# Gate sums moved to TensorE, row loads to SyncE's queue, and the small steps of the maxima spread over ScalarE and GpSimd

## The chip, the cores and the metric

The kernel runs on one NeuronCore of a Trainium2 chip. The core has four computing engines, each with its own in-order queue of instructions: TensorE (PE in the profile, its weight loads PEld) multiplies matrices into PSUM, VectorE (DVE), ScalarE (ACT) and GpSimd (POOL) work elementwise and reduce. SyncE (SP) issues DMAs; ScalarE and GpSimd can issue DMAs too, and an instruction that issues one waits in that engine's queue like any other. The metric is the device time of one execution in microseconds. A program on one core has no second core to wait for, so the time is the span of this core's instructions and a little around it.

## The reference

For an input x of 2048 rows and 512 columns the kernel computes a gated mix of two layers, in float32:

```python
g = sigmoid((x * gate_w).sum(-1, keepdims=True))
q, k, v = split(x @ wqkv)              # 32 heads of 16 columns each
a = (softmax(q @ k.T * 16 ** -0.5) @ v) @ wo        # per head, then the output matrix
b = Cr @ (x @ Wr.T) - Ci @ (x @ Wi.T)               # real part of a Fourier transform over rows and columns
out = g * a + (1 - g) * b
```

Wr, Wi (512 x 512) and Cr, Ci (2048 x 2048) are inputs. The weights wqkv and wo are scaled up by 64, so the scores of the softmax are large: each row's maximum has to be known before the exponentials.

## The kernel before, in words

**Precision.** Most matrix products run on float32 operands that are split into two rounded halves, `hi` and `lo` (type F32R). A product is then three products, hi*hi, hi*lo and lo*hi, collected in PSUM. `split` (line 336) makes the halves: ScalarE copies to `hi`, another engine subtracts to get `lo`. `halves_of` (line 185) gives each product as two matmuls on 64 rows each, into two PSUM banks that are added at the evacuation.

**Stages.** The order of the instructions is written out by hand; no planner moves them. All of the following runs in one stream of TensorE:

1. Projections to q and k, transposed (`project_t`, line 465): 32 tiles of 128 x 512, the first nine in the list `order` (line 548). Their operands come from the transposed input xT, loaded into four tiles `raws` in quarters of 512 columns, and from the first columns of wqkv. Every tile is evacuated from PSUM (ScalarE, then DVE or POOL), split into `eh` and `el`, and stored to DRAM (`q_d`, `k_d`).
2. Projections to the values (`project_s` with `wv`, 16 tiles, about 115.7 to 184.4 us). In the same stretch the gate's sums are made: for each block of 128 rows, `load_xn` (line 569) loads x through SP, `gate_sum` (line 573) multiplies it with the gate's row, broadcast to all partitions in `gb`, on POOL, and ScalarE sums the product over its columns into `z`. `gates` (line 589) turns z into g and 1 - g.
3. The two column transforms (`project_s` with `wr`, then `wi`, 16 tiles each, to about 314.5 us), stored to DRAM (`ab_d`), and `fold_keys` (line 412), which makes sums and differences of key columns.
4. The row transforms (88 groups of 24 matmuls, to about 683 us). Their coefficients `craw` are loaded by SP eight groups ahead into five buffers, and split by POOL (`prepare`, line 363).
5. The attention of 16 pairs of heads, one after another, with the rest of the row transforms and the output matrix beside it.

**Scans beside the stages.** The maxima of the scores are found beside stages 1 to 4. A scan multiplies a block of queries with a block of keys (line 139 for the first pair, line 158 after it); DVE, or ScalarE and DVE together (a fold: lines 162 and 164), reduce the result to the maxima `mx`. Every step of three products advances a count of slots (`beside`, line 292). Work is put a number of slots later by `after(n, f)`, and a scan is given out every few slots (PACE 3.9, BESIDE 2.72, PART 2.07 slots a scan), independent of the time that passes.

**Row loads.** The scans of a pair of heads need rows of q and k, which `row_loads` (line 93) brings from DRAM into two tiles of the ring `stk` (six buffers) with eight DMAs. `load_scan_beside` (line 284) puts them seven slots apart, beginning 28 scans before the pair starts (24 for the second pair). For the first pair they are issued by SP, for the other pairs by ScalarE. In the row transforms a pair's 64 scans are 132 slots, a group of 24 matmuls 12 slots.

**The end of a pair.** `shift` (line 167) reduces the maxima once more, transposes them (both DVE), splits them into `hi` and `lo` (lines 181 and 182, both DVE, 128 x 32 elements), and SP stores both. The five parts come three slots after the pair's last scan and then every four slots. For one pair, `PART_PAIR`, the tile of maxima is first filled by a memset on POOL (line 155).

**Evacuation of the natural-order tiles.** `project_s` (line 495) multiplies one bank of the result by a sign into `tx` on ScalarE. For odd tiles after the first 64 scans DVE adds the other bank from PSUM; for the others ScalarE evacuates it too (`ty`, line 506) and POOL adds.

Of the kernel before, what the change touches and what calls it, by code (L numbers as in the profile page):

```python
# [10 lines left out]
F32 = mybir.dt.float32  # L11
# [7 lines left out]
P = 128  # L19
# [33 lines left out]

def build(tc, x, xT, wqkv, wo, wrT, wiT, cr, ci, gate, out):
    nc = tc.nc
    with ExitStack() as ctx:
# [88 lines left out]
        def scan_folded(n, j, bank, pool):  # L145

            p, i = SEQ[n]  # L150
            qb, c = i // 4, i % 4
            if i == 0 and j == 0:
                new_maxima(p)
                if p == PART_PAIR:
                    nc.gpsimd.memset(mx[p], -3.0e38)
            qs, ks = scanned[p]
            b, ps = 64 * j, bank(f"{'dk'[c % 2]}{j}")
            nc.tensor.matmul(ps, qs[b:b + 48, qb * P:(qb + 1) * P], ks[b:b + 48, c * 512:(c + 1) * 512],  # L158
                             start=True, stop=True)
            if c % 2 == 0:  # L160
                fold[j] = pool.tile([P, 512], F32, tag=f"fold{j}", name="fold")
                nc.scalar.activation(fold[j], ps, AF.Relu)  # L162
            else:
                nc.vector.tensor_tensor_reduce(out=fold[j], in0=ps, in1=fold[j], scale=1.0, scalar=-3.0e38,  # L164
                                               op0=ALU.add, op1=ALU.max, accum_out=mx[p][:, j, qb, c // 2:c // 2 + 1])

        def shift(p):

# [5 lines left out]
            def store():  # L174
                for n, s in enumerate((hi, lo)):
# [4 lines left out]
                    lambda: nc.vector.transpose(t, m),  # L180
                    lambda: nc.vector.tensor_copy(hi, t),
                    lambda: nc.vector.tensor_sub(lo, t, hi.bitcast(F32)),
                    store]
# [71 lines left out]
        with ExitStack() as pf:  # L255
# [28 lines left out]
            def load_scan_beside(p):  # L284
                scanned[p], loads = row_loads(p, nc.scalar if p else nc.sync, kf_d if p else k_d)
                for n, load in enumerate(loads):
                    after(7 * n, load)
# [4 lines left out]
            def beside():  # L292
# [6 lines left out]
                while seen[0] < FRONT and pace[1] >= 1.0:  # L299
# [16 lines left out]
                    if done is not None and SEQ[done][1] == SCANS - 1:  # L316
                        for d, part in enumerate(shift(SEQ[done][0])):
                            maxima.append(part)
# [64 lines left out]
            with ExitStack() as px:  # L383
# [28 lines left out]
                def fold_keys(f, g):  # L412

                    a, b = (ep.tile([P, 512], F32, tag="el", name="fa") for _ in range(2))
                    c = 2 * g
# [30 lines left out]
                def difference(f, c, s):  # L446
# [5 lines left out]
                    kept.clear()  # L452
                    hi = ep.tile([P, 512], F32R, tag="dh", name="dh")
                    lo = a.bitcast(F32R)
# [10 lines left out]
                def project_t(w, dst, f, c, ps=None):  # L465
# [6 lines left out]
                    hi = ep.tile([P, 512], F32R, tag="eh", name="eh", bufs=3)  # L472
                    lo = ep.tile([P, 512], F32R, tag="el", name="el")
                    nc.scalar.copy(tx, ps[0])
# [20 lines left out]
                def project_s(w, t, sign, use):  # L495
# [5 lines left out]
                    nc.scalar.mul(tx, ps[0], sign)  # L501
                    if beds and t % 2 and t < NB - 1:
                        after(4, use, t, tx, ps[1], nc.vector.tensor_add if sign > 0 else nc.vector.tensor_sub)
# [20 lines left out]
                for d in range(ND):  # L524
                    nc.sync.dma_start(raws[d][:, q4[0]], xT[d * P:(d + 1) * P, q4[0]])
                    nc.sync.dma_start(rq[d][:, near], wqkv[d * P:(d + 1) * P, near])
                load_cols(1, near)
                for c in range(1, NC):
                    load_x(c)
                for i in range(2):  # L530
                    load_cols(i, far)
                nc.sync.dma_start(ones_d.rearrange("a (b c) -> (a b) c", c=32), ones)
                gb = ep.tile([P, D], F32, tag="gb", name="gb", bufs=1)
                after(200, nc.sync.dma_start, gb, gate.to_broadcast([P, D]))

# [6 lines left out]
                for d in range(ND):  # L542
# [3 lines left out]
                    for c in range(1, NC):  # L546
                        after(24 * c - 6 + 4 * d, split_x, d, c)
                order = [(wq, q_d, 0, 0), (wk, k_d, 0, 0), (wq, q_d, 1, 0)]
                order += [(w, dst, 0, c) for c in range(1, NC) for w, dst in ((wq, q_d), (wk, k_d))]
                for n, (w, dst, f, c) in enumerate(order):  # L550
                    lead = s1() if n in (0, 2, 4, 6) else None
                    project_t(w, dst, f, c, lead and (lead[:, 0, :], lead[:, 1, :]))
                after(22, load_scan_beside, 0)
                after(84, scan_at, PACE)
# [11 lines left out]
                wr = new_cw()  # L566
                xn = {}

                def load_xn(t):
                    xn[t] = rp.tile([P, D], F32, tag="raw", name="xn")  # L570
                    nc.sync.dma_start(xn[t], x[t * P:(t + 1) * P, :])

                def gate_sum(t):
                    xg = ep.tile([P, D], F32, tag="el", name="xg")
                    nc.gpsimd.tensor_mul(xg, xn.pop(t), gb)
                    after(7, lambda: nc.scalar.activation(xg, xg, AF.Copy, accum_out=z[:, t:t + 1]))

                def to_values(t, tx, ps, add):
# [3 lines left out]
                for t in range(NB):  # L582
                    load_xn(t)
                    after(30 if t < NB - 1 else 18, gate_sum, t)
                    if t == 2:
# [525 lines left out]
```

## Time and profile before

| | |
|---|---|
| time, median of 3 runs | 1749.48 us (1747.13 to 1753.26) |
| the profiled execution | 1751.22 us, its span 1749.4 us |
| instructions | 36091 |
| TensorE busy | 1720.8 us (98%) |
| ScalarE busy | 1518.9 us (87%) |
| VectorE busy | 1098.3 us (63%) |
| GpSimd busy | 676.6 us (39%) |
| mean granted TensorE clock | 0.998 |
| HBM read / written | 134.09 MB / 61.61 MB |

The profile is of one execution. Its views: groups of instructions by line and engine (busy time, mean of one, and what ended the idle time before them), the busy time of each engine in windows, the waits by who waited for whom, the chain of work that ended last, and the timeline. A row of the timeline has the start and the length in microseconds, the engine (with a q for its queue: a DMA that it issues), the line of the kernel, the operation, what is written from what, and in brackets the engine's idle time before it and what released it. The ends of matmuls are modelled: a busy TensorE is not TensorE at its peak, so the number of matmuls in a stretch says more than its busy time.

### The profile page before, as it was taken

How to read it: one execution, taken by the hardware profiler on the slowest of the kernel's cores; microseconds unless marked ns; L12 is line 12 of the kernel's file. 1: busy time of each engine (PE TensorE's matmuls, PEld its weight loads, DVE VectorE, ACT ScalarE, POOL GpSimd, SP SyncE). 2: the span in 40 equal slices, each digit the busy share in tenths (PEclk: the TensorE clock that was granted, in tenths of full speed). 3: DMA queues.
4: the chain of work that ended last, by engine and by line, in shares of the span. 5: the costliest groups of instructions: out<-in, count | busy, mean ns of one | idle time of the engine just before them, and what ended most of it. 6: DMA issues, size and time to landing. Idle time of an engine off the chain costs nothing.

```text
span 1749.4 us, 36091 instructions
## 1 busy us (share of the span) xinstructions
PE 1720.8 (98%) x13640; PEld 1034.4 (59%) x13640; DVE 1098.3 (63%) x2074; ACT 1518.9 (87%) x2514; POOL 676.6 (39%) x784
## 2 busy tenths in 40 slices
PE   8999999999999999999999999999999999999998
PEld 7877788888888787333333333333455555555554
DVE  6897788899998987666666666666521222222333
ACT  5448888888887887999999999999988888888885
POOL 3576444755554764032423223232322322223212
PEclk9999999999999999999999999999999999999999
DMA  7783556443446836144243323242234254255612
GB/s 262 238 275 89 177 174 190 145 117 110 117 116 157 198 107 126 25 78 81 39 84 58 63 60 66 54 85 57 50 91 96 56 122 90 69 139 142 173 39 100
DMA packets 125630, 197.48 MB, mean 113 GB/s; under 512 B 53856, under 2 KB 56400, under 8 KB 118544
## 3 DMA queue, kind: packets, MB, share of 16 engines
q1 hardware_dynamic: 82864, 157.35, 33.7%
q0 software_dynamic: 38496, 19.47, 5.4%
q10 hardware_dynamic: 4096, 18.36, 4.1%
q8 instruction: 107, 1.75, 0.5%
q14 instruction: 67, 0.55, 0.1%
HBM read 134.09 MB, written 61.61 MB: 112 GB/s over the span
## 4 chain that ended last, share of the span: by engine, by line
PE 89%; ACT 3%; DVE 2%; issue 2%; POOL 2%; DMA 2%; SPq 0%; ACTq 0%; DVEq 0%; POOLq 0%
PE pvb L752 28%; PE xy L189 19%; PE s L214 18%; PE s L189 10%; PE s L158 9%; PE s L139 4%; DVE fold L164 1%; ACT fold L162 1%; POOL s L282 1%; POOL el L282 1%; ACT ty L506 0%; DMA xn<-x 0%; DMA early<-ab_d 0%; ACT eh L282 0%; DVE s L282 0%
## 5 line engine op out<-in xcount | busy, mean ns | idle before, releaser
L238 ACT ACTIVATE eb<-s 128x1024 f32<-128x1024 f32 x512 | 577.6, 1128 | 65.3 <-PE s L214 65.2
L246 ACT ACTIVATE e<-s 128x512 f32<-128x512 f32 x1022 | 608.0, 707 | 0.4 <-PE s L214 0.4
L141 DVE TENSOR_REDUCE mx<-s 128x2 f32<-128x1024 f32 x364 | 442.6, 1225 | 192.6 <-PE s L139 192.4
L752 PE MATMUL pvb<-eb,va 128*17 128x512 f32 x2052 | 513.0, 597 | 0.0
L752 PE MATMUL pvb<-e,va 128*17 128x512 f32 x2044 | 512.1, 597 | 0.0
L164 DVE CUSTOM_DVE_ANT_0 fold<-s,fold 128x512 f32<-128x512 f32 x660 | 443.5, 690 | 67.4 <-ACT fold L162 28.6
L162 ACT ACTIVATE fold<-s 128x512 f32<-128x512 f32 x660 | 386.6, 602 | 78.6 <-PE s L158 49.3
L214 PEld LDWEIGHTS s<-qs,ks 50*128 50x128 f32 x2048 | 214.1, 184 | 355.4 <-ACT eb L238 255.1
L214 PE MATMUL s<-qs,ks 50*128 50x512 f32 x2048 | 420.5, 435 | 0.0
L189 PE MATMUL xy<-b,c 64*128 64x512 f32 x2448 | 397.7, 393 | 0.6 <-ACT s L478 0.6
L158 PE MATMUL s<-ks,qs 48*128 48x512 f32 x1320 | 328.9, 407 | 12.2 <-ACT fold L162 6.4
L189 PEld LDWEIGHTS xy<-b,c 64*128 64x128 f32 x2448 | 281.3, 187 | 20.1 <-ACT s L478 2.7
L158 PEld LDWEIGHTS s<-ks,qs 48*128 48x128 f32 x1320 | 181.1, 184 | 70.1 <-ACT fold L162 21.5
L771 POOL DMA_DIRECT2D r_d<-lc x31 | 18.1, 583 | 456.0 <-DVE lc L770 456.0
L752 PEld LDWEIGHTS pvb<-eb,va 128*17 128x17 f32 x2052 | 70.5, 96 | 191.1 <-issue 183.7
L139 PE MATMUL s<-ks,qs 48*128 48x512 f32 x728 | 152.6, 394 | 1.4 <-DMA qs<-q_d 0.7
L764 POOL DMA_DIRECT2D lc<-ob x124 | 62.9, 514 | 154.0 <-DVE ob L761 153.7
L189 PE MATMUL xy<-w,b 64*128 64x512 f32 x768 | 119.1, 394 | 1.9 <-ACT ty L506 1.7
L369 POOL TENSOR_TENSOR c<-craw,c 128x512 fp32r<-128x512 f32 x84 | 109.9, 1308 | 6.7
L189 PE MATMUL s<-b,chi 64*128 64x512 f32 x670 | 105.3, 390 | 0.3 <-ACT chi L1065 0.3
L368 POOL CAST c<-craw 128x512 fp32r<-128x512 f32 x84 | 51.8, 617 | 133.1 <-PE xy L189 126.1
L189 PEld LDWEIGHTS xy<-w,b 64*128 64x128 f32 x768 | 85.9, 186 | 13.9 <-ACT ty L506 2.1
(132 smaller groups left out, 1524.0 us busy)
## 6 DMA issues: line engine op xcount, KB each, us to landing
craw<-ci SPq DMA_DIRECT2D x64, 256.0 KB
craw<-cr SPq DMA_DIRECT2D x60, 256.0 KB
ks<-k_d SPq DMA_DIRECT2D x44, 256.0 KB
qs<-q_d SPq DMA_DIRECT2D x44, 256.0 KB
ab_d<-ab SPq DMA_DIRECT2D x32, 256.0 KB
y_d<-y SPq DMA_DIRECT2D x32, 256.0 KB
o_d<-oh POOLq DMA_DIRECT2D x28, 256.0 KB, 13.2
o_d<-ol POOLq DMA_DIRECT2D x28, 256.0 KB, 13.7
```

The source lines that it names most:

```text
L139: nc.tensor.matmul(ps[:, j, :], qs[b:b + 48, qb * P:(qb + 1) * P], ks[b:b + 48, c * 512:(c + 1) * 512], start=True, stop=True)
L141: nc.vector.tensor_reduce(mx[p][:, :, qb, c], ps, axis=AX.X, op=ALU.max)
L158: nc.tensor.matmul(ps, qs[b:b + 48, qb * P:(qb + 1) * P], ks[b:b + 48, c * 512:(c + 1) * 512], start=True, stop=True)
L162: nc.scalar.activation(fold[j], ps, AF.Relu)
L164: nc.vector.tensor_tensor_reduce(out=fold[j], in0=ps, in1=fold[j], scale=1.0, scalar=-3.0e38, op0=ALU.add, op1=ALU.max, accum_out=mx[p][:, ...
L189: nc.tensor.matmul(ps[j], lhs[r], rhs[r], start=first, stop=last)
L214: nc.tensor.matmul(pss[j], ks[b:b + 50, kb * P:(kb + 1) * P], qs[b:b + 50, q0:q0 + 512], start=True, stop=True)
L238: nc.scalar.activation(e, ps, AF.Exp, scale=SCALE)
L246: nc.scalar.activation(e[j], pss[j], AF.Exp, scale=SCALE)
L369: sub(lo, raw, hi.bitcast(F32))
L752: nc.tensor.matmul(pvb[r:r + VC, :], va[:, kb, 2 * p + j, :], es[c][j], start=kb == 0, stop=kb == NB - 1, tile_position=(0, r))
L764: nc.gpsimd.dma_start(lc[32 * n:32 * n + 32, :], ob[r + DH:r + VC, :].rearrange("p (s e) -> p s e", e=16))
```

## The change

- The gate's sums are made by TensorE: x times the gate vector is a product of a block of the transposed input (128 x 128, as weights) with a column of the gate (128 x 1), four of them collected for 128 rows. `gate_sums(c)` does this for 512 rows, 16 matmuls in plain float32, and ScalarE copies the four columns to `z`. It is called behind the projections number 0, 3, 5 and 7 of `order`. The gate vector is loaded once as 128 x 4 elements by SP, between the first loads. The loads of x, the broadcast gate `gb`, the products on POOL and the sums on ScalarE go, and the input x with them.
- All row loads are issued by SP.
- The tag `el` has four buffers in place of two; `dh` takes the single buffer that `gb` had.
- In `project_s`, DVE adds for two tiles of three in place of one of two.
- In the maxima's end beside the stages, `hi` is copied by ScalarE and `lo` subtracted by POOL; the memset of `mx` moves from POOL to DVE.

```diff
                 if p == PART_PAIR:
-                    nc.gpsimd.memset(mx[p], -3.0e38)
+                    nc.vector.memset(mx[p], -3.0e38)
...
-        def shift(p):
+        def shift(p, copy=nc.vector.tensor_copy, sub=nc.vector.tensor_sub):
...
-                    lambda: nc.vector.tensor_copy(hi, t),
-                    lambda: nc.vector.tensor_sub(lo, t, hi.bitcast(F32)),
+                    lambda: copy(hi, t),
+                    lambda: sub(lo, t, hi.bitcast(F32)),
...
-                scanned[p], loads = row_loads(p, nc.scalar if p else nc.sync, kf_d if p else k_d)
+                scanned[p], loads = row_loads(p, nc.sync, kf_d if p else k_d)
...
-                        for d, part in enumerate(shift(SEQ[done][0])):
+                        for d, part in enumerate(shift(SEQ[done][0], nc.scalar.copy, nc.gpsimd.tensor_sub)):
...
-                    a, b = (ep.tile([P, 512], F32, tag="el", name="fa") for _ in range(2))
+                    a, b = (ep.tile([P, 512], F32, tag="el", name="fa", bufs=4) for _ in range(2))
...
-                    hi = ep.tile([P, 512], F32R, tag="dh", name="dh")
+                    hi = ep.tile([P, 512], F32R, tag="gb", name="dh", bufs=1)
...
-                    lo = ep.tile([P, 512], F32R, tag="el", name="el")
+                    lo = ep.tile([P, 512], F32R, tag="el", name="el", bufs=4)
...
-                    if beds and t % 2 and t < NB - 1:
+                    if beds and t % 3 and t < NB - 1:
...
                 load_cols(1, near)
+                gc = sm.tile([P, ND], F32, tag="gc", name="gc", bufs=1)
+                nc.sync.dma_start(gc, gate.rearrange("o (d p) -> p (o d)", p=P))
                 for c in range(1, NC):
                     load_x(c)
...
-                gb = ep.tile([P, D], F32, tag="gb", name="gb", bufs=1)
-                after(200, nc.sync.dma_start, gb, gate.to_broadcast([P, D]))
...
+                def gate_sums(c):
+
+                    ps = s1()
+                    for j in range(4):
+                        for d in range(ND):
+                            nc.tensor.matmul(ps[:, 0, j:j + 1], raws[d][:, (4 * c + j) * P:(4 * c + j + 1) * P],
+                                             gc[:, d:d + 1], start=d == 0, stop=d == ND - 1)
+                    nc.scalar.copy(z[:, 4 * c:4 * c + 4], ps[:, 0, 0:4])
+
                 order = [(wq, q_d, 0, 0), (wk, k_d, 0, 0), (wq, q_d, 1, 0)]
                 order += [(w, dst, 0, c) for c in range(1, NC) for w, dst in ((wq, q_d), (wk, k_d))]
                 for n, (w, dst, f, c) in enumerate(order):
                     lead = s1() if n in (0, 2, 4, 6) else None
                     project_t(w, dst, f, c, lead and (lead[:, 0, :], lead[:, 1, :]))
+                    if n in (0, 3, 5, 7):
+                        gate_sums(c)
...
-                def load_xn(t):
-                    xn[t] = rp.tile([P, D], F32, tag="raw", name="xn")
-                    nc.sync.dma_start(xn[t], x[t * P:(t + 1) * P, :])
-
-                def gate_sum(t):
-                    xg = ep.tile([P, D], F32, tag="el", name="xg")
-                    nc.gpsimd.tensor_mul(xg, xn.pop(t), gb)
-                    after(7, lambda: nc.scalar.activation(xg, xg, AF.Copy, accum_out=z[:, t:t + 1]))
...
                 for t in range(NB):
-                    load_xn(t)
-                    after(30 if t < NB - 1 else 18, gate_sum, t)
```

More of the change, by code (lines that the diff above doesn't have):

```diff
@@ L51, with build @@
 AHEAD = (30, 31, 37, 44)
-def build(tc, x, xT, wqkv, wo, wrT, wiT, cr, ci, gate, out):
+def build(tc, xT, wqkv, wo, wrT, wiT, cr, ci, gate, out):
     nc = tc.nc
@@ L566, in build @@
                 wr = new_cw()
-                xn = {}
-                def load_xn(t):
-                    xn[t] = rp.tile([P, D], F32, tag="raw", name="xn")
-                    nc.sync.dma_start(xn[t], x[t * P:(t + 1) * P, :])
-                def gate_sum(t):
-                    xg = ep.tile([P, D], F32, tag="el", name="xg")
-                    nc.gpsimd.tensor_mul(xg, xn.pop(t), gb)
-                    after(7, lambda: nc.scalar.activation(xg, xg, AF.Copy, accum_out=z[:, t:t + 1]))
                 def to_values(t, tx, ps, add):
@@ L1092 @@
     arrays = {
-        "x": np.ascontiguousarray(x),
         "xT": np.ascontiguousarray(x.T),
```

## The prediction

> **What bounds the kernel now.** I read the page's busy table first, then the busy time by window, because a share of the span says nothing about a single stage. The windows' columns are: stretch, its length, then busy time and (number of instructions) of PE, PEld, DVE, ACT and POOL, granted clock, DMA share, GB/s.
>
> ```profile
> PE 1720.8 (98%) x13640; PEld 1034.4 (59%) x13640; DVE 1098.3 (63%) x2074; ACT 1518.9 (87%) x2514; POOL 676.6 (39%) x784
> ```
>
> ```profile
> 11.00:33.30 22.30, 22.09 (x194) 17.76 (x192) 17.02 (x25) 15.71 (x33) 8.83 (x7) 1.00 0.84 309
> 33.30:35.90 2.60, 0.34 (x4) 0.03 (x1) 2.28 (x3) 1.04 (x4) 1.24 (x1) 0.99 0.48 185
> 35.90:39.30 3.40, 3.40 (x16) 2.93 (x18) 0.69 (x1) 1.61 (x3) 2.11 (x2) 0.50 0.45 170
> 115.70:145.30 29.60, 26.15 (x213) 19.92 (x215) 24.54 (x26) 14.10 (x29) 20.81 (x17) 1.00 0.81 226
> 145.30:184.40 39.10, 36.84 (x298) 28.31 (x296) 30.06 (x87) 35.46 (x75) 21.99 (x18) 1.00 0.27 80
> 184.40:194.00 9.60, 8.35 (x69) 6.18 (x67) 5.97 (x18) 8.57 (x20) 5.06 (x4) 1.00 0.39 108
> 194.00:250.60 56.60, 55.84 (x464) 46.76 (x462) 47.52 (x138) 48.10 (x92) 26.70 (x21) 1.00 0.63 198
> 250.60:314.50 63.90, 63.30 (x530) 54.77 (x528) 52.13 (x154) 56.76 (x108) 32.58 (x27) 1.00 0.66 195
> 314.50:683.00 368.50, 362.75 (x3009) 310.70 (x3007) 337.10 (x993) 309.76 (x542) 210.48 (x208) 1.00 0.50 132
> ```
>
> ```profile
> 475.00:500.00 25.00, 25.00 (x216) 22.41 (x215) 23.33 (x69) 21.36 (x37) 12.54 (x14) 1.00 0.41 117
> 750.00:775.00 25.00, 25.00 (x190) 9.02 (x182) 17.33 (x17) 25.00 (x41) 4.89 (x10) 1.00 0.46 82
> ```
>
> TensorE is the bound almost everywhere, and from 683 us on (the attention steps, the last row) it has no gap that a changed line could fill: the change touches only the first 683 us. There the count of matmuls shows what the busy time hides. The best stretch does 216 in 25 us, 0.1157 us each. At that rate each stretch loses its length minus its count times 0.1157: the projection of the values 5.0 and 4.6 us (115.7 to 184.4), the stretch behind it 1.6, the first transform 2.9, the second 2.6, the long spectral stretch 20.4. Only these losses, and the 4 us around 35 us, can be won; an added matmul, where TensorE stands full, adds its own time.
>
> **The gate's sums on TensorE.** Added: 64 matmuls of 128x128 weights on one column, 16 behind each of projections 0, 3, 5 and 7, four small copies on ScalarE, one load of 2 KB.
>
> ```profile
> L538 PE MATMUL s<-ident 128*128 128x128 f32 x20 | 4.2, 404 | 1.4 <-POOL ident masks.py:199 1.4
> L1050 PE MATMUL s<-ob,sel 128*128 128x256 f32 x4 | 1.1, 405 | 0.0
> 10.64 1.33 ACT L337 CAST c<-raws 128x256 fp32r<-128x256 f32 x4 [0.88 <-DMA raws<-wqkv]
> r_d<-lc POOLq DMA_DIRECT2D x31, 8.0 KB, 1.7
> 35.90 9.36 PE L189 MATMUL xy<-b,w 64*128 64x512 f32 x66 [2.26 <-DVE s L282]
> ```
>
> No row has this shape. The transposes cost 4.2/20 = 0.21 us with 128 columns at the very start: the upper end. The four of L1050 are (1.1 - 0.4)/3 = 0.23 us apart with 256 columns, so 0.11 with 128; one column can't cost more, and I take that, since the weights are as large. The lower end is half of it, 0.055. So 64 cost 7.0 (3.5 to 13.4). I add 0.8 for eight changes between matmul shapes (an estimate, 0 to 1.6) and 0.7 for the gate's load: it stands in SP's queue behind the wqkv load that ScalarE still waits for at 10.64, and the first sums are due at 11.1; the small load of r_d takes 1.7 from issue, hence 0 to 1.7. Behind it in SP's queue stand the 12 loads of the other input columns, each one issue later; their first matmuls come two projections (some 5 us) after the point where TensorE is at 11.1, so this costs nothing. The four copies wait in ScalarE's queue for the sums, with casts and evacuations behind them; its idle 6.6 of the 22.3 us from 11.0 hide that, and without them projection 2 or 3 would start late.
>
> Against this, TensorE now stands still from 33.3 to 35.9 (DVE's sum `s` is late behind the weight splits) and then gets half the clock: 16 matmuls in 3.4 us, 1.5 more than at the full rate. The extra 1.8 us before each of projections 4, 6 and 8 gives DVE that time, so I count 2.3 + 1.5 = 3.8 as covered (lower end 2). Net 8.5 - 3.8 = +4.7 (-0.3 to +15).
>
> The Trainium skill, "TensorE: Matmul & The Clock Gate", Part 1, says that idle TensorE windows of about 3.4 us halve the clock; this case's trace agrees with one halving of 3.4 us, behind a stop of 2.3. Read strictly, it speaks against the change; the clock rival below works this out from rows.
>
> **What the removed sums free.** Gone are 16 loads of x, the gate's 256 KB load, 16 POOL products and 16 ScalarE sums.
>
> ```profile
> 129.00:193.00 64.00, 11.52 (x32) 20.62 (x16) 1.00 0.38 103
> 120.42 0.49 SPq L571 DMA_DIRECT2D xn<-x  x1
> 126.62 0.31 ACTq L104 DMA_DIRECT2D qs<-q_d  x1
> 128.62 0.74 PE L189 MATMUL xy<-w,b 64*128 64x512 f32 x4 [1.66 <-ACT ty L506]
> 140.01 0.62 ACT L337 CAST c<-wraw 128x512 fp32r<-128x512 f32 x1 [2.39 <-DMA wraw<-wrT]
> 143.29 0.50 PE L158 MATMUL s<-ks,qs 48*128 48x512 f32 x2 [1.09 <-ACT fold L162]
> SPq L425 <- ACT xg L576: 13.5, 2, 13.3
> ```
>
> The first row holds the sums alone: 11.52 us of ScalarE, 20.62 of POOL. ScalarE is 35.46 of 39.1 us busy there, 91%, and TensorE waits for its folds. Two stops have other roots in the same lines: at 126.62 ScalarE was held in a row load until the x load issued at 120.42 had landed, and TensorE lost 1.66; the weights wrT, queued in SP behind x loads, stopped ScalarE 2.39 at 140.01, and TensorE 1.09 at 143.29. All go. I leave this stretch the loss rate of the first transform, 2.9/56.6 = 5%, 3.4 of its 9.6: -6.2 (-3 to -8). From 184.4 to 194 the last two sums and SP's 13.3 us wait for `el` go: 1.6 less 5% gives -1.1. The `el` ring of four brings nothing beyond that, and `dh`, now in one buffer, nothing to pay: its two uses are two projections apart.
>
> **Eight more tiles added by DVE.** t % 3 for t % 2 makes 26 instead of 18.
>
> ```profile
> L603 DVE TENSOR_TENSOR ab<-tx,xy 128x512 f32<-128x512 f32 x14 | 9.6, 684 | 0.0
> L506 ACT ACTIVATE ty<-xy 128x512 f32<-128x512 f32 x30 | 18.0, 601 | 0.9 <-POOL va L579 0.9
> ```
>
> That is 8 x 0.684 = 5.5 us more DVE and 8 x 0.601 = 4.8 less ScalarE (and as many additions less on POOL) between 145 and 314, where the windows have DVE 80% and ScalarE 88% busy. DVE then stands at 83%. I cost it at nothing, between a gain of half of ScalarE's 4.8 and a loss of half of DVE's 5.5: DVE's slack covers it, and where it doesn't, DVE's folds come late and TensorE waits for their banks.
>
> **The maxima's split and the memset off DVE and POOL.**
>
> ```profile
> 469.57 1.11 DVE L182 TENSOR_TENSOR clo<-mt,chi 128x32 fp32r<-128x32 f32 x1
> 471.34 0.50 PE L158 MATMUL s<-ks,qs 48*128 48x512 f32 x2 [0.66 <-DVE mx L164]
> 0.00:690.00 690.00, 4.33 (x11) 1.00 0.56 163
> 0.00:690.00 690.00, 5.07 (x11) 1.00 0.56 163
> 621.71 0.69 DVE L164 CUSTOM_DVE_ANT_0 fold<-s,fold 128x512 f32<-128x512 f32 x1 [1.50 <-POOL mx L155]
> 622.46 0.50 PE L158 MATMUL s<-ks,qs 48*128 48x512 f32 x2 [1.09 <-DVE mx L164]
> ```
>
> The two windows count L181 and L182 alone: 11 pairs, 9.4 us of DVE, which is 91% busy from 314.5 on. One of them, 1.11 us long, ends in a stop of 0.66. I take 0.3 of the 9.4, -2.8 (0 to -5.6): on the way ScalarE's copy may wait for DVE's transpose with folds behind it, and SP's store waits for POOL, behind it coefficient loads eight groups ahead of their use. The memset removes its own 1.09: -1.1.
>
> **Row loads from ScalarE's queue to SP's.** 88 issues move. On ScalarE, 84% busy from 314.5 on, an issue of 0.31 us (at 366.54 below) fits into the idle time and is worth nothing; what goes is the hold.
>
> ```profile
> 547.04 0.31 ACTq L104 DMA_DIRECT2D qs<-q_d  x1
> 548.10 0.50 PE L158 MATMUL s<-ks,qs 48*128 48x512 f32 x2 [0.96 <-ACT fold L162]
> 366.54 0.31 ACTq L104 DMA_DIRECT2D qs<-q_d  x1
> 368.35 0.33 SPq L361 DMA_DIRECT2D craw<-cr  x1
> 370.60 0.61 PE L158 MATMUL s<-ks,qs 48*128 48x512 f32 x2
> 561.66 0.47 PE L158 MATMUL s<-ks,qs 48*128 48x512 f32 x1 [0.65 <-issue]
> 53.29 5.19 DMA qs<-q_d
> SPq L361 <- POOL c L369: 247.9, 74, 4.4
> ```
>
> At 547 such a hold cost 0.96: -1.0. The price is in SP. Each coefficient load waits there for POOL (last row), and by the program's slots a pair's last row load is emitted just behind one, in slots 1 to 3 of its 12 in five of six pairs. In the case shown it would leave not at 366.54 but behind 368.35, at 368.7. Its second half is first read by the pair that starts at 370.60. With 1.7 for a small landing and 1.0 for the 256 KB ahead of it in the same queue (at some 260 GB/s, as in the first windows) it lands at 371.4: 0.8 late. One that landed as slowly as the SP load at 53.29 (5.2) would be 3.3 late; one that takes 1.7 is in time. At 561.66 TensorE already waits so. Over six pairs that is 6 x 0.75 = +4.5 (0 to 20).
>
> The Trainium skill, "DMA: Bandwidth & Descriptors", section "Issuing engines are not separate DMA queues", says that the issuing engine matters only for issue time, since all DMAs share 16 engines. By that the term would be about 0 and the sum -7.5; no run so far shows SP and ScalarE with the same load.
>
> **Sum.** +4.7 - 6.2 - 1.1 + 0 - 2.8 - 1.1 - 1.0 + 4.5 = -3.0 us. The profiled execution took 1751.22 us (span 1749.4 and 1.8 around it), so 1748.2; it was 1.7 above the median of 1749.48, on which the sum gives 1746.5.
>
> **Rivals.**
> *The row loads are in time and the thin matmuls cheap* (faster): 4.5 falls away, and 64 x 0.055 saves 3.5: -11.0, 1738.5. For it: the load at 366.54 had 4 us and caused no stop. Against: 561.66. Chance 0.27.
> *SP's queue makes every pair late* (the other side): each of six last loads lands as at 53.29, 3.3 late, 20 instead of 4.5: +12.5, 1762. For it: 247.9 us of SP waits and a DMA share of 0.50. Against: 368.7 needs only 1.9 to be in time. It decides for slower (over +5.2) from 2.1 us a pair. Chance 0.13.
> *The clock halves behind each block of sums*: four times the 1.5 of 35.9, +6: +3, 1752.5. For it: the halving behind 33.3. Against: a block is 1.8 us, and the stop of 1.66 at 128.62 had none. Chance 0.12.
>
> **How the numbers follow.** My forecast has 0.48; its own range is 1741 to 1752. A measurement of this kernel can tell about 0.3% (5.2 us) from no change. Faster: 0.27 and a third of the forecast's 0.48, 0.42. Slower: 0.13 and 0.02 of the tails, 0.15. Same: 0.43. The range 1737 to 1756 takes in the first rival and the clock's, and leaves out SP's.
>
> **What would show it.** The sums: 16 matmuls in some 1.8 us after 11 us, no stop at 33.3 and clock 1.00 there. Values: no waits for wraw or row loads on ACT, and 115.7 to 184.4 shorter by 6. Split: no PE stop behind a pair's switch of DVE. Rows: PE waits of 0.5 to 1 us at the first scans of a pair, released by a row load of SP. The prediction is wrong if those waits are absent or over 2 us, if a sum costs far from 0.11, or if DVE's folds become what TensorE waits for between 194 and 314.

## The result, and the profile after

The changed kernel takes 1775.59 us (median of 4 runs, 1775.08 to 1776.05) against 1750.62 for the kernel before (median of 4, 1747.13 to 1753.26): the ratio is 1.0144, with a 95% interval of 1.0125 to 1.0163. It is 25 us slower, where the forecast was 3 us faster and the range ended at 1756.

The first line of the profile's busy table, after:

```profile
PE 1746.3 (98%) x13768; PEld 1067.0 (60%) x13768; DVE 1095.7 (62%) x2061; ACT 1508.3 (85%) x2489; POOL 647.8 (37%) x770
```

POOL has lost 29 us and ScalarE 11, but neither sets the time. TensorE has 25.5 us more, and 128 more instructions for 64 added products.

Stages are compared by the same marks in every kernel: the starts of ScalarE's evacuations of transposed projections 0, 8 and 31, of the last value tile, of the last tile of either transform, and of the last tile of the spectral stretch. The busy time between these marks, first of the kernel before, then of the one after (columns as in the prediction's windows):

```profile
11.90:36.30 24.40, 21.96 (x190) 17.59 (x188) 18.48 (x26) 16.26 (x33) 10.07 (x7) 0.99 0.79 290
...
118.60:184.60 66.00, 60.28 (x489) 46.02 (x486) 52.11 (x110) 49.20 (x104) 40.49 (x32) 1.00 0.48 134
184.60:251.10 66.50, 64.49 (x531) 53.29 (x529) 53.70 (x157) 56.97 (x112) 31.76 (x25) 1.00 0.59 186
...
315.50:676.40 360.90, 355.38 (x2949) 305.00 (x2947) 329.96 (x973) 303.12 (x530) 207.35 (x205) 1.00 0.50 132
```

```profile
11.60:57.40 45.80, 45.80 (x315) 39.37 (x316) 19.02 (x26) 17.39 (x37) 10.22 (x8) 0.78 0.46 166
...
137.60:196.50 58.90, 58.14 (x490) 49.04 (x489) 52.01 (x110) 40.99 (x78) 20.80 (x17) 1.00 0.44 120
196.50:259.40 62.90, 62.90 (x531) 56.53 (x528) 53.99 (x158) 54.04 (x104) 25.84 (x21) 1.00 0.54 163
...
323.70:699.80 376.10, 361.75 (x2949) 312.04 (x2947) 325.74 (x959) 303.17 (x537) 208.81 (x211) 0.98 0.48 127
```

Two stretches got longer. The front, 24.4 us before, takes 45.8, at a mean clock of 0.78. The spectral stretch goes from 360.9 to 376.1 with the same 2949 matmuls. Two got shorter: the values by 7.1, and the first transform from 66.4 to 62.9, where TensorE is now busy all the time.

The chain of work that ended last shows what fills both losses (start, length, what):

```profile
10.64 4.57 PE s L553 x32
15.21 5.23 PE xy L189 x24
20.44 2.76 PE s L189 x24
...
25.93 3.66 PE s L553 x32
29.59 4.53 PE s L189 x24
...
376.31 3.89 DMA qs<-q_d
...
526.41 4.24 DMA qs<-q_d
573.66 8.63 DMA ks<-kf_d
```

L553 is the gate's sums. A block has 32 instructions where the code has 16 products. At the full clock it takes 3.66 us, 0.114 per instruction and 0.229 per product; the first one, 4.57, runs into a stretch of half clock from 13.27 on. The half of a projection right behind a block (24 instructions of L189) takes 5.23 and 4.53, the next one 2.76. Further down, row loads have come onto the chain, each with some 4 us or more from issue to use.

How long each stretch is in every kernel that was run (us, from the profiled execution; "rest" is the attention; the numbers are those of the experiments below; there is no 11):

| kernel | start | proj. 0-8 | proj. 8-31 | values | 1st transform | 2nd | spectral | rest | span |
|---|---|---|---|---|---|---|---|---|---|
| before | 11.9 | 24.4 | 82.3 | 66.0 | 66.4 | 64.4 | 361.0 | 1072.9 | 1749.4 |
| after | 11.6 | 45.9 | 80.2 | 58.8 | 62.9 | 64.3 | 376.2 | 1073.9 | 1773.7 |
| 1 row loads on ScalarE | 11.6 | 46.1 | 79.6 | 58.9 | 63.1 | 64.4 | 362.3 | 1073.8 | 1759.7 |
| 2 no sums | 11.8 | 24.5 | 80.8 | 58.8 | 62.9 | 64.5 | 375.3 | 1073.2 | 1751.8 |
| 3 sums spread | 11.6 | 38.5 | 81.6 | 58.8 | 62.9 | 64.3 | 374.7 | 1073.8 | 1766.3 |
| 4 row loads earlier | 11.2 | 46.0 | 80.2 | 58.9 | 64.4 | 64.4 | 355.2 | 1073.7 | 1754.0 |
| 5 before, row loads on SP | 11.4 | 25.2 | 81.6 | 62.7 | 66.5 | 64.4 | 377.2 | 1073.2 | 1762.2 |
| 6 before, POOL's sums early | 11.6 | 25.0 | 95.5 | 58.8 | 63.0 | 64.3 | 361.4 | 1072.5 | 1752.2 |
| 7 before, maxima only | 11.2 | 25.1 | 81.3 | 63.2 | 66.4 | 64.4 | 361.0 | 1072.8 | 1745.4 |
| 8 before, tiles only | 11.3 | 25.3 | 81.4 | 63.8 | 66.6 | 64.9 | 362.6 | 1072.5 | 1748.4 |
| 9 POOL's sums moved, rows early | 11.2 | 25.2 | 82.5 | 61.6 | 66.4 | 64.6 | 354.4 | 1073.4 | 1739.2 |
| 10 split, rows early | 11.6 | 24.4 | 81.9 | 62.6 | 67.8 | 64.5 | 354.7 | 1073.2 | 1740.7 |
| 12 wide matmuls between | 11.6 | 48.7 | 80.9 | 58.9 | 62.9 | 64.3 | 377.8 | 1073.8 | 1778.9 |

### The profile page after: what moved, and what is told of

The parts are those of the page before. It is cut to its first block, busy times and chain, and to the rows that moved or that the text cites. A ratio compares the mean times of both kernels' runs of the same rounds, so it can differ in the third digit from the quotient of the medians.

```text
span 1773.7 us, 36238 instructions
## 1 busy us (share of the span) xinstructions
PE 1746.3 (98%) x13768; PEld 1067.0 (60%) x13768; DVE 1095.7 (62%) x2061; ACT 1508.3 (85%) x2489; POOL 647.8 (37%) x770
## 4 chain that ended last, share of the span: by engine, by line
PE 91%; DVE 2%; DMA 2%; POOL 2%; issue 1%; ACT 1%; SPq 0%; DVEq 0%; POOLq 0%; ACTq 0%
PE pvb L750 28%; PE xy L189 22%; PE s L214 18%; PE s L189 10%; PE s L158 9%; PE s L139 4%; DVE mx L141 1%; PE s L553 1%; POOL s L282 1%; DMA ks<-kf_d 0%; DVE fold L164 0%; DMA qs<-q_d 0%; POOL el L282 0%; DMA abr<-ab_d 0%; DMA gc<-gate 0%
## 5 line engine op out<-in xcount | busy, mean ns | idle before, releaser
L189 PE MATMUL xy<-b,c 64*128 64x512 f32 x2448 | 410.6, 402 | 0.7 <-ACT s L478 0.6
L158 PE MATMUL s<-ks,qs 48*128 48x512 f32 x1320 | 329.4, 411 | 15.6 <-issue 8.5
L189 PEld LDWEIGHTS xy<-b,c 64*128 64x128 f32 x2448 | 294.1, 192 | 21.2 <-ACT s L478 2.8
L158 PEld LDWEIGHTS s<-ks,qs 48*128 48x128 f32 x1320 | 182.8, 186 | 65.8 <-issue 13.9
L762 POOL DMA_DIRECT2D lc<-ob x124 | 62.9, 514 | 157.2 <-DVE ob L759 157.1
L189 PE MATMUL xy<-w,b 64*128 64x512 f32 x768 | 117.0, 393 | 0.2 <-ACT s L478 0.2
L189 PE MATMUL s<-b,chi 64*128 64x512 f32 x670 | 105.9, 392 | 0.3 <-ACT chi L1063 0.3
L189 PEld LDWEIGHTS xy<-w,b 64*128 64x128 f32 x768 | 83.9, 186 | 10.8 <-ACT s L478 1.1
```

The lines of the kernel that those rows point to most:

```text
L189: nc.tensor.matmul(ps[j], lhs[r], rhs[r], start=first, stop=last)
L762: nc.gpsimd.dma_start(lc[32 * n:32 * n + 32, :], ob[r + DH:r + VC, :].rearrange("p (s e) -> p s e", e=16))
```

## The experiments

The theory after the result: the sums cost some 20 us, by their own time and by the clock behind them, and the late row loads as much again; the rest of the change gains what was expected of it. The rivals are that one of the two carries nearly all, or that the gains are absent and smaller losses stand in several places.

**1. Row loads back on ScalarE's queue.**

```diff
-                scanned[p], loads = row_loads(p, nc.sync, kf_d if p else k_d)
+                scanned[p], loads = row_loads(p, nc.scalar if p else nc.sync, kf_d if p else k_d)
```

> The changed kernel with one part undone: row loads in ScalarE's queue again. Theory (last row loads of a pair leave SP too late, behind a coefficient load that waits for POOL): the long waits at the first scans of pairs 1, 2, 3, 8 and 9 go (19.4 us in the stages they lie in) and the half clock behind them, the old hold of ScalarE near 547 us comes back (about 1.5): some 1757.5 us. Rival (the maxima's split over ScalarE and POOL makes the pairs' switches late): the waits stay, 1774 to 1777 us.

1757.05 us, ratio 1.0037 (1.0022 to 1.0052). The spectral stretch falls from 376.2 to 362.3 and nothing else moves by more than 0.6. Against the 1.0144 of the whole change, the move to SP costs 0.0107, 18.7 us. The stage shows less, 13.9, because this profiled execution (1761.54) is 4.5 us above the median: one switch of pairs, at 569.9, still waits 2.5 us in it, with half clock behind.

**2. The sums left out.**

```diff
-                    if n in (0, 3, 5, 7):
-                        gate_sums(c)
...
+        nc.vector.memset(z, 0.0)
```

> The changed kernel without the 64 matmuls and four copies of the gate (z is zero, so the gate is one half everywhere; the gate's load stays). Theory (the sums cost TensorE their own time, 128 instructions of 0.114 us = 14.6, 16.0 with their starts, and half clock after each of four blocks, about 7.5, against a stop of 3.8 that comes back behind projection 8): 19 to 20 us less, 1756 us. Rival (the gate's load and the copies in ScalarE's queue are what costs): a start that is still several us later than before's, 1765 us or more.

1755.44 us, ratio 1.0026 (1.0017 to 1.0036). The front is back at 24.5, and the 2.6 us stop of the kernel before is there again, with half clock behind it at 35.4 us. The sums cost 0.0118, 20.7 us, and they did cover that stop. The two together are 39 us where 25 were lost, so the rest of the change gains some 14. Neither of the two carries nearly all.

**3. The same 64 products, four at a time.**

```diff
-                    if n in (0, 3, 5, 7):
-                        gate_sums(c)
...
+                for k in range(16):
+                    after(14 + 7 * k, gate_sums, k // 4, k % 4)
```

> The changed kernel with the same 64 sums given out four at a time, every seven slots, between the matmuls of projections 1 to 9, in place of four blocks of 16. Theory with the clock (blocks of thin matmuls of 3.7 us halve the clock): the halvings before 60 us go and their 7 us with them, the sums' own 15 us stay: 1768 to 1769 us. Rival (their own time is all that matters): 1775 us, and the same time between the first projection and 76 us as in the changed kernel.

1768.85 us, ratio 1.0100 (1.0083 to 1.0117). The front takes 38.5 instead of 45.9, and the clock stays full there. Two of the sixteen groups now come behind projection 8, so the first two stages have to be taken together: 126.1 us after, 120.1 here, 105.3 without the sums. So 6.0 of the sums' 20.8 us go with the half clock (6.7 by the medians), and 14.8 stay. That is near to 128 instructions at 0.114, 14.6. But a group of eight holds TensorE a little longer, 0.98 us (from 19.88 to 20.86), 15.7 in all, and the stop that the sums cover is set against it.

What decides on the clock is seen when a stretch is cut where the clock changes. After, instructions of the projections alone (L189; columns: stretch, length, PE, PEld, granted clock, DMA share, GB/s; the number counts every instruction that touches the stretch, up to four more than start in it):

```profile
9.85:13.27 3.42, 0.35 (x4) 0.03 (x2) 1.00 1.05 384
13.27:16.68 3.41, 1.54 (x8) 1.26 (x10) 0.50 1.04 368
16.68:20.09 3.41, 3.41 (x20) 2.67 (x18) 0.50 1.07 370
20.09:23.51 3.42, 3.42 (x34) 2.98 (x32) 1.00 0.60 212
26.92:30.33 3.41, 0.81 (x8) 0.69 (x10) 1.00 0.30 112
30.33:33.74 3.41, 3.41 (x20) 2.67 (x18) 0.50 0.19 68
```

In this trace the clock changes only at steps of 3.41 us. A piece of that length in which few wide matmuls run (4, 8 and 8 here; the rest of it is filled with gate sums) is followed by one at half the clock. A piece full of projections at half the clock has 20, and is followed by full clock, with 34. The Trainium skill, "TensorE: Matmul & The Clock Gate", Part 1, describes a free-running window of 3413 ns; the trace agrees (13.27 to 30.33 is five of them). What these rows add is that a TensorE busy with one-column products counts for that window about as one that stands still.

**12. A wide matmul between every four sums.** This asks whether a run of thin matmuls has to be long, or whether their share counts.

```diff
                                              gc[:, d:d + 1], start=d == 0, stop=d == ND - 1)
+                        if j < 3:
+                            nc.tensor.matmul(ps[:, 1, :], wq[0][j][:, 0:P], xs[j, 0][0], start=True, stop=True)
```

> The kernel after, with one matmul of 128x128 weights on 512 columns (a product already computed, its result is not read) put between every four gate sums of a block, three in each block, twelve in all, 0.24 us each at the full clock: 2.8 us of added work. A block is then four pieces of 1.0 us of thin matmuls with 0.24 us of wide ones between them. Theory 1 (the clock halves where thin matmuls alone run for 2.7 to 3.7 us; a wide one in between starts the count anew): no half clock behind the blocks, their some 6 us of loss go, 2.8 are added: 1772 us (1770 to 1774). Theory 2 (the clock follows the share of thin work in a fixed stretch of 3.4 us, which stays near 80%): the clock halves behind the blocks as before, and some of the added matmuls run at half of it: 1779 us (1778 to 1781).

1780.24 us, ratio 1.0175 (1.0153 to 1.0197). The front gets 2.8 longer, and the clock is halved for as many pieces as before, six. That fits the share, as the second theory had it. Pieces of this kernel ahead of a halved one, and then pieces of experiment 3 with the most sums in them, all matmuls together (columns as in the stages' windows):

```profile
11.67:15.08 3.41, 3.41 (x29) 3.27 (x30) 1.18 (x3) 0.48 (x2) 0.00 (x0) 1.00 1.05 388
25.32:28.74 3.42, 3.42 (x29) 3.29 (x30) 1.18 (x1) 0.34 (x1) 0.63 (x1) 1.00 0.50 190
```

```profile
11.62:15.03 3.41, 3.41 (x29) 2.85 (x29) 2.80 (x5) 2.21 (x5) 1.28 (x1) 1.00 1.07 390
42.34:45.75 3.41, 3.41 (x29) 2.81 (x29) 1.39 (x2) 1.20 (x4) 1.19 (x1) 1.00 0.40 154
```

All four have 29 matmuls and no gap. In the first two, 24 instructions of the gate's sums start; in the last two 13 and 14, and there the clock stays.

**4. SP's queue kept, row loads issued earlier.**

```diff
-ROWS = {SCANS * n + (36 if n else 40): p for n, p in enumerate(EARLY[1:])}
-ROWS.update({SCANS * len(EARLY) - 54: PART_PAIR, SCANS * len(EARLY) - 24: len(EARLY)})
+ROWS = {SCANS * n + (28 if n else 40): p for n, p in enumerate(EARLY[1:])}
+ROWS.update({SCANS * len(EARLY) - 54: PART_PAIR, SCANS * len(EARLY) - 29: len(EARLY)})
```

> The changed kernel, row loads still in SP's queue, but begun eight scans (some 6 us) earlier in the pair before (five for the pair after PART_PAIR). Theory (only the lateness of the last loads costs, not the queue): the waits at the switches go and the hold of ScalarE stays away, 19 us less: 1756 us. Rival (SP's queue is behind by more than any head start, or the loads hold up the coefficients behind them): under 8 us less, 1768 us or more.

1755.49 us, ratio 1.0027 (1.0017 to 1.0036). The spectral stretch takes 355.2: 21.0 less than after, and 5.8 less than before. So it is not the queue as such that costs, but that its loads come too late. TensorE's waits in that stretch (waited for: us in total, times, longest), after and with the loads earlier:

```profile
PE s L158 <- issue: 8.5, 3, 4.5
PE s L158 <- DMA qs<-q_d: 4.0, 2, 2.1
PE s L158 <- ACT fold L162: 1.2, 2, 1.0
PE s L158 <- DVE mx L164: 0.5, 2, 0.2
```

```profile
PE s L158 <- ACT fold L162: 0.5, 2, 0.3
PE s L158 <- DVE mx L164: 0.5, 2, 0.3
```

The waits for "issue" and for the row load go, 12.5 us in five stops. Three of them, 8.5 us, are put down to "issue", that is to nothing that the profile shows; since they go with the earlier loads, they too were waits for rows. The timeline of one of the five late loads, after, first SP's queue, then TensorE:

```profile
375.92 0.34 SPq L361 DMA_DIRECT2D craw<-cr  x1
376.31 0.43 SPq L104 DMA_DIRECT2D qs<-q_d  x1
```

```profile
378.17 0.43 PE L158 MATMUL s<-ks,qs 48*128 48x512 f32 x1
380.44 0.47 PE L158 MATMUL s<-ks,qs 48*128 48x512 f32 x1 [1.84 <-DMA qs<-q_d]
380.44 0.93 PE L189 MATMUL xy<-b,c 64*128 64x512 f32 x4
```

And the same load with earlier slots:

```profile
368.37 0.35 SPq L361 DMA_DIRECT2D craw<-cr  x1
368.77 0.43 SPq L104 DMA_DIRECT2D ks<-kf_d  x1
369.24 0.42 SPq L104 DMA_DIRECT2D qs<-q_d  x1
```

As predicted, the row load leaves SP right behind the coefficient load. It then takes until 380.2 to land (the chain's 3.89), and the scan due at 378.6 starts at 380.44. The last load of experiment 4 leaves at 369.24, 7 us earlier, and lands in time. The stop has a second part: the piece of 3.41 us that it falls into has few matmuls, so the next one runs at half the clock. That happens at 381.9, 480.9, 532.1 and 583.3 (twice), and accounts for the 0.98 in the stage's row. So 12.5 of the 21.0 are waits, and the other 8.5 go with these five pieces.

**5. The kernel before with only the row loads moved.**

```diff
-                scanned[p], loads = row_loads(p, nc.scalar if p else nc.sync, kf_d if p else k_d)
+                scanned[p], loads = row_loads(p, nc.sync, kf_d if p else k_d)
```

> The kernel before with one part of the change alone: all row loads in SP's queue. Theory (the loads' place in SP behind the coefficient loads is enough by itself): the five stops at the switches come in full (about 19), the two holds of ScalarE go (1.8 near 126 us, 1.5 near 547 us): 16 us more, 1766 us. Rival (the stops need SP's store of the maxima waiting for POOL as well): under 8 us more, 1758 us or less.

1765.17 us, ratio 1.0088 (1.0067 to 1.0109). That is 15.3 us more, as the theory had it: the split of the maxima is not needed for the stops. The spectral stretch gets 16.2 longer (361.0 to 377.2). The values get 3.3 shorter, part of which is the hold near 126 us that goes.

**7. The kernel before with the maxima's split and the memset.**

```diff
-                        for d, part in enumerate(shift(SEQ[done][0])):
+                        for d, part in enumerate(shift(SEQ[done][0], nc.scalar.copy, nc.gpsimd.tensor_sub)):
...
-                    nc.gpsimd.memset(mx[p], -3.0e38)
+                    nc.vector.memset(mx[p], -3.0e38)
```

> The kernel before with the maxima's hi on ScalarE and lo on POOL beside the stages, and the memset on DVE, alone. By the prediction's terms 2.8 and 1.1 less: 1746.6 us. The changed kernel's stages behind the switches that were late before (0.9 and 1.6 less, two others) point to 3 less, 1747.5 us. Rival (ScalarE waits for the transposes and gives it back): 1750 us.

1746.72 us, ratio 0.9977 (0.9966 to 0.9988): the time expected, but not where. The stage table has the spectral stretch at 361.0 as before, and 2.8 us less in the values. TensorE's waits in the spectral stretch, before and here:

```profile
PE s L158 <- DVE mx L164: 3.1, 6, 1.1
PE s L158 <- ACT fold L162: 1.4, 3, 1.0
PE s L158 <- issue: 0.6, 1, 0.6
```

```profile
PE s L158 <- issue: 2.7, 1, 2.7
PE s L158 <- ACT fold L162: 2.3, 3, 1.8
PE s L158 <- DVE mx L164: 0.5, 2, 0.3
```

The split does what was said of it: the waits for DVE at the ends of pairs fall from 3.1 to 0.5. With that time saved TensorE comes earlier to the last pair, whose row load was only just late before (0.6), and waits 2.7 there, with half clock behind it. So in this execution the gain is handed back at the next late thing. How much of the 2.7 comes from the time saved is not shown: experiment 8, with the maxima as before, waits 1.6 at the same place. The gain appears once the rows are early: 355.2, 354.4 and 354.7 in experiments 4, 9 and 10. Where the 3.1 us lie by which the medians differ, one profile of each kernel can't show.

**8. The kernel before with only the eight more tiles.** (`t % 2` becomes `t % 3`.)

> The kernel before with the eight more tiles added by DVE alone. By the prediction nothing: 1750 us. If ScalarE is what holds the values and transforms back (it was 88 to 91 per cent busy), 2 to 4 us less, 1747 us; if DVE becomes it, 2 to 3 us more.

1750.45 us, ratio 1.0006 (0.9993 to 1.0019): no difference. Its values take 63.8, like 62.6 to 63.2 in experiments 5, 7 and 10, though the gate's sums are where they were in all four. So the 66.0 of the profiled execution before holds some 2 to 3 us that other executions of the same work do not have.

**6. POOL's sums kept, but moved to the projections.** The kernel before with the maxima's split, the memset and `t % 3`; loads of x and sums, made in place in the loaded rows, at slots from 102 and 126 on, one every 10.

```diff
+                for t in range(NB):
+                    after(102 + 10 * t, load_xn, t)
+                    after(126 + 10 * t, gate_sum, t)
...
-                    load_xn(t)
-                    after(30 if t < NB - 1 else 18, gate_sum, t)
```

> The kernel before, its gate sums still made by POOL and ScalarE from loads of x, but given out beside the projections of q and k (every ten slots from slot 126, about 43 to 82 us), where POOL and ScalarE are about half busy; with the two-of-three tiles, the maxima's split and the memset of the change; row loads in ScalarE's queue. Theory (the gain of the values' stretch comes from ScalarE and POOL being free of the sums there, wherever they go): 7 from the values, 3 from the stretch behind, 2 to 3 from maxima and memset: 1738 us. Rival (the sums crowd POOL and ScalarE in the projections and cost there what they save): 1746 us or more.

1751.16 us, ratio 1.0006 (0.9995 to 1.0017): the theory's 1738 was wrong, and the time is in the rival's range. Values and first transform gain as after (58.8 and 63.0), but projections 8 to 31 take 95.5 instead of 82.3. Busy time from 75 to 100 us, before and here; then, here, the chain of work between 70 and 104 us by line with its longest piece, and TensorE's longest stop:

```profile
75.00:100.00 25.00, 24.83 (x211) 20.54 (x207) 24.68 (x24) 11.43 (x21) 17.77 (x15) 1.00 0.77 273
```

```profile
75.00:100.00 25.00, 20.09 (x160) 14.10 (x156) 16.09 (x16) 11.62 (x27) 18.86 (x16) 0.98 0.72 239
```

```profile
by line: POOL el L282 25.6%; DMA q_d<-el 25.5%; POOL s L282 24.3%; POOL xn L556 16.9%; issue 8.8%; ACT eh L282 1.9%; POOLq L282 0.3%; POOLq L338 0.1%
...
86.16 8.66 DMA q_d<-el
```

```profile
101.28 0.79 PE L189 MATMUL xy<-b,c 64*128 64x512 f32 x2 [5.01 <-DVE s L282]
```

POOL is 75% busy, where it was 71% before (not about half, as the expectation had it), and TensorE does 160 matmuls instead of 211. Within this stretch the chain runs through POOL: its steps for the terms and the gate's products (`xn`) follow each other without a gap up to 88.9. Then it stands still until 94.97, since its next tile's buffer is held by a store that took 8.66 us; behind that DVE's sum is late, and TensorE stops for 5.0. That stop, and the half clock from 98.8 to 105.6 that it brings, are over half of the 13.2 lost. So the rival, crowding, has a slow store on top of it. Why the store took so long was not traced, and the two were not separated: the ring `el` has two buffers here, and no run gave it four.

**10. The parts that gain, with the row loads early.** The kernel before with the edits of experiments 5 and 7 and the slots of experiment 4.

> The kernel before with the maxima split by ScalarE and POOL, the memset on DVE, and all row loads in SyncE's queue but 8 scans earlier (5 for the last pair); sums, values and tiles as before. Theory (the queue costs nothing once the loads are issued 8 scans earlier, and the holds of ScalarE at the row loads near 126 and 547 us go): -3.3 for the maxima and the memset, -1.2 at the pair switches, -1.5 at 547, -3.4 in the values by the hold near 126, so 1741 us (1739 to 1743). Rival (the queue itself costs time, whatever the slot: the coefficient loads behind the row loads come late): no better than the maxima alone, 1746 or above.

1742.53 us, ratio 0.9967 (0.9954 to 0.9979), against 1747.78 before in these runs. That is 5.3 us faster, where the expectation, reckoned from 1750, was 9: the spectral stretch gained 6.3, as the theory has it, and the values gained only against the one profile of before.

**9. The same, with POOL's sums in other slots.** Experiment 10 with `t % 3`, and the sums made in place in the loaded rows at chosen slots.

```diff
+GATES = (244, 260, 276, 386, 400, 414, 428, 442, 456, 470, 484, 498, 512, 526, 540, 554)
...
+                for t, at in enumerate(GATES):
+                    after(at - 24, load_xn, t)
+                    after(at, gate_sum, t)
```

> The kernel before with the parts of the change that gained (maxima split by ScalarE and POOL, memset on DVE, t % 3), all row loads in SyncE's queue but 8 scans earlier (5 for the last pair), and the gate's sums left on POOL and ScalarE, made in place in the loaded rows, three of them at slots 244 to 276 and thirteen every 14 slots from 386 on, the last ones so behind the values. Theory (TensorE is the bound, and its added 16 us of thin matmuls and the late row loads were the whole loss): -3.3 for the maxima and the memset, -1.2 at the pair switches with the rows early, -1.5 at the stop at 547, and some 4 of the 7 us in the values, so 1740 us (1737 to 1743). Rival (crowding: the sums cost TensorE time wherever POOL and ScalarE are filled with them, as between 60 and 100 us with the sums at slots 126 to 276): 1746 or above.

1737.39 us, ratio 0.9941 (0.9926 to 0.9956): 10.4 us faster than before, and the best of all. Its values and its spectral stretch:

```profile
118.90:180.50 61.60, 58.75 (x489) 48.06 (x487) 52.03 (x110) 47.90 (x103) 36.91 (x30) 1.00 0.63 170
311.40:665.80 354.40, 353.13 (x2950) 308.45 (x2948) 324.82 (x960) 302.99 (x538) 208.92 (x212) 1.00 0.52 134
```

TensorE stands still for 2.9 us in the values and 1.3 in the spectral stretch, without one added matmul. Against experiment 10 the medians differ by 5.1 and the profiled executions by 1.5; where the rest lies was not traced.

## Why the prediction was wrong

**The price of a sum.** The step that failed is "The four of L1050 are (1.1 - 0.4)/3 = 0.23 us apart with 256 columns, so 0.11 with 128; one column can't cost more". The 0.11 is right for an instruction (0.114), but a product in plain float32 is two instructions: 64 products are 128, 14.6 us instead of 7.0, and above the stated upper end of 13.4. The kernel before could have shown it, by the count of a group set against the products in its line of code: L1050 is one product in a loop over two halves, and the profile has it four times. The 0.11 read from it was half a product.

**The clock behind the blocks.** The rival was described rightly and given 0.12, because "a block is 1.8 us". A block is 3.7 us. Its price of 6 us came out, 6.0 by the stages and 6.7 by the medians when the sums are spread, though six pieces were halved and not the four that it counted. The reading of the quoted stop also missed the unit: what counts is how much wide work falls into a piece of 3.41 us, not whether TensorE stands still.

**What the sums cover.** Right: the stop at 33.3 and the half clock behind it are gone after and in experiment 3, and back in experiment 2. Over the first two stages the kernel after takes 19.4 more than before (21.5 in the front less 2.1 behind it), instead of the term's 4.7. Experiment 2 puts the sums at 20.8, since projections 8 to 31 are 1.5 shorter without them too. With the late row loads (below) this makes the error, in about equal parts.

**The values.** -6.2 predicted, -7.1 measured on the same profile, and the waits that were named are gone. Against the other profiles of the same work it is -4 to -5.

**Behind the values.** -1.1 predicted, -3.5 measured. The first transform's loss of 2.9 was taken as its usual rate; experiment 6 has the same 63.0 with neither POOL's sums in that place nor the ring of four, so the sums were the cause there, and the ring is not needed for it; `t % 3` alone (experiment 8) leaves 66.6. Every run without POOL's sums there has `t % 3`, so whether the gain needs both is not shown.

**Tiles, maxima, memset, hold.** Zero for the tiles: right, 1.0006. The three others were -4.9 together; the spectral stretch is 5.8 to 6.6 shorter where the rows come in time. What the prediction did not say is what is late next, the last pair's rows.

**The row loads.** The mechanism is the predicted one, with the place in SP's queue that was worked out. The step that failed is "With 1.7 for a small landing and 1.0 for the 256 KB ahead of it in the same queue [...] it lands at 371.4: 0.8 late". Here that load took 3.9 from issue to landing in place of 2.7, and two others on the chain 4.2 and 8.6; why was not traced. Four switches waited 1.84 to 2.14 and one 4.46, instead of 0.75 each, and the half clock behind the stops had no place in the term. Instead of 4.5, the late switches cost 21.0 together against rows that are early (experiment 4); against rows in ScalarE's queue, with which the prediction compared, the stretch is 16.2 longer, with the hold of ScalarE already taken off (experiment 5). The rival built on the row at 53.29 (5.2) was right on the side and, with its 20 us, on the size. The size is in part luck: its stops of 3.3 are too long for four of the five, and the clock is missing from it too. By the Trainium skill, "DMA: Bandwidth & Descriptors", section "Issuing engines are not separate DMA queues", the term would have been about 0. Experiment 5 shows 16.2 us instead, and the measurement decides; with the loads issued earlier from the same queue (experiment 4) nothing of it is left.

Stage by stage, 14.7 more for the first two stages (19.4 for 4.7), 15.6 more for the spectral stretch (15.2 for -0.4, which was 4.5 for the rows less 4.9) and 3.3 less for the values and the stretch behind them turn the prediction's -3.0 into +24.0; the two spans differ by 24.3. The two rivals were priced as if only one could come true. They lie in different stretches and share no cause, so nothing kept them from adding up.

## What to carry to other kernels

Set the number of records in a group against the products in its line before a duration is taken from it, and ask of thin matmuls not only what they take but what share of a clock window they fill: four products at a time between wide work left the clock full, sixteen in one block did not. A DMA moved to another engine's queue needs its slot moved too: the margin is from the issue that the new queue allows to the first use, by a landing taken from a load of that size in that stretch. A stall that goes shows its worth only if what was just in time behind it is brought forward as well.

## What the runs showed of the hardware

A float32 product of 128x128 weights with one column takes two TensorE instructions of 0.114 us. The single column gains nothing over the 0.1157 us at which matmuls of 64 rows on 512 columns follow each other.

Over the profiles of all these kernels, cut into pieces of 3.41 us on the grid of the clock's changes (from 8 to 690 us), every piece at full clock in which 10 or fewer wide matmuls started (37 pieces) was followed by half clock, none with 15 or more (some 2450) was, and of those with 11 to 14 ten of 19 were. A full piece has about 29, a halved one mostly 16, which is 1.5 us of work less. Whether the rest of the piece was a stop or one-column products made no difference. So a stop of 2 us can cost 1.5 us more than itself, or not, by where it falls on the grid: after, those of 1.84 and 2.06 us before 380.44 and 480.20 lie inside one piece and were followed by half clock, and the one of 1.95 before 431.23, across the boundary at 429.69, was not.
